# A build-time list scheduler gets landing times by kind of DMA and a new priority table

## Chip, core and metric

The kernel runs on one core of one Trainium2 chip. The metric is the device time of one execution in microseconds; the kernel before was run three times. The chip has five engines that each work through a queue of their own in order: TensorE (PE, with its weight loads PEld), VectorE (DVE), ScalarE (ACT), GpSimd (POOL) and SyncE (SP), which here only starts DMAs.

## What is computed

Three layers in a row. (1) Attention in which a query sees only the keys of its own cluster (the nearest of 16 centroids); B=2, H=8, S=768, D=64. (2) A mixture of experts on the 1536 tokens of width 512: a gate of softmax over 8 experts picks one expert per token. (3) A dense layer 512 to 2048 to 512 with a leaky activation.

```python
mask = q_assign[:, :, :, None] == k_assign[:, :, None, :]
attn = softmax(where(mask, q @ k.T / 8, -1e9)); x = attn @ v          # (1)
e_idx = argmax(x @ w_gate + modality_bias[modality_id])
y = gate_w * (relu(x @ w1[e_idx]) @ w2[e_idx])                          # (2)
h = y @ w_in; out = (max(h, 0) + alpha * min(h, 0)) @ w_out             # (3)
```

## The kernel before

**Who sets the order.** The kernel body doesn't issue instructions. It describes its operations with `S.op(...)` (engines that could do it with an estimated cost on each, buffers read and written, a priority, a tag), and `Sched.run` (lines 194 to 309) plans them when the program is built: it keeps a planned clock for each engine, takes the operation that can start first, and among those of one engine that can start within a small window of each other the one with the lowest priority number. `emit` then issues them in that order. On the chip each engine's queue runs in exactly this order and waits where data is late, so the plan's estimates decide the order and the chip decides the time. `ORDER` (line 79) adds a number to the priority of each tag.

**How the planner sees a DMA.** All DMAs share one planned clock, `dma_free`. In `run` (lines 281 to 286) a DMA that starts at `st` ends its transfer at `max(st + ISSUE, dma_free) + xfer`, with `xfer` given at the operation, and lands 0.13 later; `LEAD` says when SP is free again. Lines 247 and 248 hold back one kind, the loads of q, k and v and of expert weights:

```python
if o.dma is not None and o.dma[1] == "load":
    at = max(at, dma_free - self.back)      # back = 2.13
```

`ISSUE` is 2.37 for a DMA transpose, 1.86 for others on SP and 1.9 for POOL's; `LEAD` is 2.91 and 5.8 (lines 102, 103). A transpose (tag `turn`, xfer 1.91, SP busy 1.43) that starts at st therefore puts `dma_free` at st + 4.28 or later and frees SP at st + 1.5.

**Attention** (`group_prep` line 714, `unit` line 957). Work goes in 8 groups (4 per batch row, 2 heads each). `group_prep` loads q, k, v (line 725, one v buffer `vraw` for all groups), transposes q and k on PE, splits them in high and low parts, finds the clusters, and moves halves between partitions (`move`, line 830: by DMA on SP, or by ACT or POOL). Each group has 12 units of 128 queries: scores on PE (L973), row maximum on DVE (L980), exp on ACT (L992), split of p into two fp16 halves (on ACT, POOL and DVE), a DMA transpose of p on SP (L1026; in the first batch row a third of the units transposes on PE instead), and the product with v on PE (L1034, L1036), which needs the group's v as two fp16 halves: vab (L916), a small chain (L922 to L935), v_hi (L394) and v_lo (L940).

**Experts** (`slot`, line 1340). Tokens are sorted by expert into tiles of 128; 5 tiles of batch row 0 and 8 of row 1 are always run, numbered m = 0 to 12. A tile gathers its rows by an indirect DMA on POOL (L1364), and issues 8 weight loads of 512 KB on SP (L1358) that are skipped on the chip when the expert is that of the tile before. Tiles 0 to 2 run in plain fp32 while attention still occupies memory (L1428 and L1458 with `wst`, about 0.6 us a matmul); they serve PE as filler. From tile 3 on, the weights are split in two parts by ACT and DVE (`whl`). Tile rows go back to memory, and a second gather (`gather`, line 1469, L1474 on POOL) with a scaling (`gated`) brings them in token order for the dense layer.

**Dense layer** (`ffn`, line 1533): the last 280 us, in which PE runs nearly without a gap (L1544, L1572). It is planned by later calls of `run` with an empty priority table (`TAIL`), but with the same DMA costs.

Of the kernel before, what the change touches and what calls it, by code (L numbers as in the profile page):

```python
# [19 lines left out]
P = 128  # L20
# [54 lines left out]
class Op:  # L75
# [16 lines left out]
class Sched:  # L92
# [9 lines left out]
    ISSUE = {"transpose": 2.37, "SP": 1.86, "POOL": 1.9}  # L102
    LEAD = {"transpose": 2.91, "SP": 5.8}
# [98 lines left out]
    def run(self, t0=0.0):  # L202
# [17 lines left out]
        dma_free = pool_till = dve_till = t0  # L220
# [3 lines left out]
        while n_done < total:  # L224
            best = None
            per = {}
            for o in ready:
# [19 lines left out]
                if o.dma is not None and o.dma[1] == "load":  # L247
                    at = max(at, dma_free - self.back)
                ch = None
                for e, c in o.eng.items():  # L250
                    st = max(at, o.at[e], free.get(e, t0))
                    if e == "DVE" and o.two:
                        st = max(st, pool_till - 0.1)
                    if e == "POOL" and not (o.dma and e in (o.dma[3:] or (e,))):
# [25 lines left out]
            moved = o.dma is not None and e in (o.dma[3:] or (e,))  # L280
            if moved:
                xfer, kind, busy = o.dma[:3]
                way = "transpose" if kind == "transpose" else e
                dma_free = max(st + self.ISSUE[way], dma_free) + xfer
                o.end = dma_free + 0.13
                free[e] = st + 1.05 if e == "POOL" else max(st + busy, o.end - self.LEAD[way])
            else:
# [4 lines left out]
                if e == "POOL":  # L292
                    pool_till = free[e]
            ready.remove(o)
# [33 lines left out]
def kernel(  # L328
# [49 lines left out]
    N = dict(s1q=2, s1k=2, s2q=2, s2k=2, p=3, p16=5, pt=4, v16=2, wf_early=2, xs=2, whl=3, whl2=3, whi='A', wlo='D', lead=1, tw=1, wdma=1.0, pss=2, ps1=4, sq=1, bd=1.5, bp=0, ulead=4, pa=2, pb=0, nat=3, hi='*', lo='DP', lo0='PPT', vraw=1, mvp=1, mvb=0, epi=1, rM=2, lob=0.5, idle=40, pace=57, mve='PA', wd=0.3, wa=0.04, wp=0.03, wpl=0.03, wsp=0.07, cs=1, back=2.13, nld=8, lump='cs', mp=90, mps=8, mpn=0, trp=0.5, evp=3, xTs2=0, xtp=9, fl=6, rsh=1, rp0=0, go=-4, so=0, pre=0, fws=5, gs=4, eb=0.8)  # L378
# [267 lines left out]
    def centroid_ops():  # L646
# [3 lines left out]
             w=[craw], dma=(0.3, True, 0.4), tag="centroid_ops1")  # L650
# [27 lines left out]
    def modality_ops():  # L678
# [3 lines left out]
            modality_id.bitcast(I32).rearrange("(b p x) -> p b x", b=B, p=P)), w=[midr], dma=(0.2, True, 0.4), tag="modality_ops1")  # L682
        S.op({"SP": 0.06}, lambda e: nc.sync.dma_start(
            mbias.t.rearrange("p m e -> p (m e)"),
            modality_bias.rearrange("(o m) e -> o (m e)", o=1).to_broadcast([P, 2 * E])), w=[mbias], dma=(0.2, True, 0.4), tag="modality_ops2")
        S.op({"SP": 0.06}, lambda e: nc.sync.dma_start(wg.t, w_gate.rearrange("(k p) e -> p k e", p=P)),
             w=[wg], dma=(0.3, True, 0.4), tag="modality_ops3")
        S.op({"SP": 0.06}, lambda e: nc.sync.dma_start(alp.t, alpha.rearrange("(f p) -> p f", p=P)),
             w=[alp], dma=(0.3, True, 0.4), tag="modality_ops4")
# [1063 lines left out]
```

## Time and profile before

| | us |
|---|---|
| three runs | 753.5, 754.52, 752.79 (median 753.5) |
| the profiled execution | 757.23 |
| its span, first to last instruction | 755.4 |
| busy in it: PE / DVE / ACT / POOL | 689.2 / 512.8 / 410.1 / 306.7 |
[...]

Read it by stages: attention up to about 300 us, experts with a long overlap from 200 to 472, the dense layer from 472 on. PE is busy in 91% of the span, so a change can win only what PE loses in gaps and at the lower clock.

### The profile page before, as it was taken

Reading aid. Unit: us, or ns where it says so; the run is one execution under the profiler, and the core shown is the slowest. Engines: PE = TensorE matmul, PEld = TensorE weight load, DVE = VectorE, ACT = ScalarE, POOL = GpSimd, SP = SyncE. Lnnn points to the kernel's source line nnn. Section 1 sums busy time; section 2 is a strip of 40 time slices with the busy share of each in tenths; the row PEclk is TensorE's granted clock in tenths of the full one; section 3 lists DMA queues with packets and bytes.
Section 4 is the critical chain, followed back from the end, with each engine's and each line's share of the span. In section 5 each row is a group of like instructions: output and inputs, shape, how many; then the busy total and the mean of one; then the engine's idle time right before and its main releaser. Section 6 shows DMA issues by size and latency. Waiting matters only on the chain. (4 is left out here: it accounts for less than half of the span.)

```text
span 755.4 us, 13680 instructions
## 1 busy us (share of the span) xinstructions
PE 689.2 (91%) x5041; PEld 581.3 (77%) x5041; DVE 512.8 (68%) x913; ACT 410.1 (54%) x624; POOL 306.7 (41%) x276
## 2 busy tenths in 40 slices
PE   8878899786998779999898897899999999999997
PEld 7767787785777655568686786799999979999996
DVE  6798888889899741799897694587777533322331
ACT  5778988787889642388776894122222341111112
POOL 4467765573667432012232100365555622222221
PEclk9999999997999989999999899799999999999999
DMA  8498899799999989913755610234433030000002
GB/s 202 127 166 186 142 212 220 131 196 234 222 191 184 174 228 171 364 62 103 267 188 184 206 56 32 85 112 127 152 112 112 28 112 1 1 0 1 1 1 84
DMA packets 167418, 101.58 MB, mean 134 GB/s; under 512 B 133136, under 2 KB 147984, under 8 KB 167344
## 3 DMA queue, kind: packets, MB, share of 16 engines
q1 hardware_dynamic: 165136, 93.63, 51.1%
q0 software_dynamic: 2208, 7.00, 3.6%
q8 instruction: 42, 0.69, 0.4%
q14 instruction: 32, 0.26, 0.1%
HBM read 87.37 MB, written 12.85 MB: 133 GB/s over the span
## 5 line engine op out<-in xcount | busy, mean ns | idle before, releaser
L1572 PE MATMUL ps<-wf,ghl 128*128 128x512 f32 x576 | 140.1, 395 | 2.4 <-POOL ghl L420 1.5
L1572 PEld LDWEIGHTS ps<-wf,ghl 128*128 128x128 f32 x576 | 107.8, 189 | 25.2 <-POOL ghl L420 3.1
L1552 DVE TENSOR_SCALAR m<-ps,alp 128x384 f32<-128x384 f32 x64 | 39.5, 617 | 126.3 <-PE ps L1544 126.3
L392 ACT ACTIVATE ghl<-g 128x384 fp32r<-128x384 f32 x64 | 33.7, 526 | 166.7 <-DVE g L1555 166.7
L420 POOL TENSOR_TENSOR p<-p,p 128x768 f16<-128x768 f32 x57 | 95.7, 1682 | 46.1 <-ACT p L392 42.1
L420 POOL TENSOR_TENSOR ghl<-g,ghl 128x384 fp32r<-128x384 f32 x63 | 67.7, 1075 | 113.9 <-ACT ghl L392 113.9
L420 DVE TENSOR_TENSOR whl<-wst,whl 128x1024 fp32r<-128x1024 f32 x80 | 96.8, 1251 | 12.9 <-ACT whl L392 12.9
L980 DVE TENSOR_REDUCE nm<-pss 128x1 f32<-128x768 f32 x96 | 91.0, 950 | 12.3 <-PE pss L973 10.9
L992 ACT ACTIVATE p<-pss,nm 128x768 f32<-128x768 f32 x96 | 86.1, 899 | 22.1 <-DVE nm L986 7.0
L392 ACT ACTIVATE whl<-wst 128x1024 fp32r<-128x1024 f32 x80 | 82.3, 1057 | 11.3 <-PE ps L1458 6.9
L1034 PEld LDWEIGHTS <-pt 128*128 128x128 f16 x1152 | 60.9, 99 | 21.7 <-DMA pt<-p 12.9
L1034 PE MATMUL ps<-v,pt 128*128 128x65 f16 x1152 | 68.9, 196 | 9.2 <-DMA pt<-p 8.1
L1544 PE MATMUL ps<-x2a,wf 128*128 128x384 f32 x384 | 73.0, 347 | 4.0 <-ACTq L1685 4.0
L1544 PEld LDWEIGHTS ps<-x2a,wf 128*128 128x128 f32 x384 | 70.4, 195 | 5.7 <-ACTq L1685 4.4
L973 PE MATMUL pss<-s1k,s1q 128*128 128x384 f32 x192 | 60.1, 395 | 16.1 <-ACT p L992 15.4
L1544 PE MATMUL ps<-x2b,wf 128*128 128x384 f32 x384 | 69.8, 338 | 0.0
L1544 PEld LDWEIGHTS ps<-x2b,wf 128*128 128x128 f32 x384 | 67.7, 188 | 1.2
L1458 PE MATMUL ps<-whl,hTs 128*128 128x512 f32 x240 | 63.1, 401 | 2.0 <-DVE hTs L420 1.2
L1428 PE MATMUL ps<-whl,xTs 128*128 128x512 f32 x240 | 63.9, 407 | 1.0 <-ACT xTs L392 1.0
L420 POOL TENSOR_TENSOR wf<-tw,wf 128x1024 fp32r<-128x1024 f32 x16 | 40.5, 2532 | 55.8 <-ACT wf L392 55.8
L1458 PEld LDWEIGHTS ps<-whl,hTs 128*128 128x128 f32 x240 | 44.5, 190 | 13.1 <-DVE hTs L420 2.4
L1428 PEld LDWEIGHTS ps<-whl,xTs 128*128 128x128 f32 x240 | 45.3, 193 | 11.3 <-ACT xTs L392 1.4
(246 smaller groups left out, 1182.8 us busy)
## 6 DMA issues: line engine op xcount, KB each, us to landing
wst<-in_moe_w_dram SPq DMA_DIRECT2D x104, 512.0 KB
wst<-in_moe_w_in_dram SPq DMA_DIRECT2D x8, 1024.0 KB
wst<-in_moe_w_out_dram SPq DMA_DIRECT2D x8, 1024.0 KB
ys_d<-ys SPq DMA_DIRECT2D x13, 256.0 KB
raw<-in_k_dram SPq DMA_DIRECT2D x8, 384.0 KB
raw<-in_q_dram SPq DMA_DIRECT2D x8, 384.0 KB
vraw<-in_v_dram SPq DMA_DIRECT2D x8, 384.0 KB
x_d<-xg SPq DMA_DIRECT2D x8, 384.0 KB
```

The costliest lines, as they stand in the source:

```text
L392: nc.scalar.activation(out=out, in_=in_, func=AF.Copy)
L420: ENG[e].tensor_tensor(out=out, in0=a, in1=b, op=ALU.subtract)
L973: nc.tensor.matmul(s.t[:, jj, 0:HS], hd["12"[i], "q"].t[:, h, j, qs], hd["12"[i], "k"].t[:, h, jj], start=(i == 0), stop=(i == 1))
L980: S.op({"DVE": c_dve(SEQ)}, lambda e: nc.vector.tensor_reduce(out=nm.t, in_=s.t[:, :, 0:HS], axis=AX.XY, op=ALU.max, negate=True), r=[s], ...
L992: S.op({"ACT": c_act(SEQ) + 0.04}, lambda e: nc.scalar.activation(out=p.t, in_=s.t[:, :, 0:HS], func=AF.Exp, bias=nm.t), r=[s, nm], w=[p], ...
L1034: nc.tensor.matmul(o[:, c], pv, vv[:, D:VW], start=(i == 0), stop=(i == 2 * C - 1))
L1428: nc.tensor.matmul(hps[jj].t, lhs(xT, a, ci), rhs(ch, w_, cols), start=(ci == 0 and i == 0), stop=(ci == 3 and i == len(parts) - 1))
L1458: nc.tensor.matmul(yp.t, lhs(hT, a, f), rhs(4 + f // 2, w_, slice((f % 2) * 512, (f % 2 + 1) * 512)), start=(f == 0 and i == 0), stop=(f = ...
L1544: nc.tensor.matmul(hp.t[:, 0:HS], wi[:, a, kk, fs], x2b.t[:, bb, kk, sl], start=(n == 0), stop=(n == 3 * KD - 1))
L1552: S.op({"DVE": c_dve(HS) + 0.055}, lambda e: nc.vector.tensor_scalar(out=m.t, in0=hp.t[:, 0:HS], scalar1=0.0, scalar2=alp.t[:, f:f + 1], o ...
L1572: nc.tensor.matmul(view(), gh.t[:, a, tt * P:(tt + 1) * P], wo[:, bb, f % 2, :], start=(f == 0 and a == 0 and bb == 0), stop=(f == NF - 1 ...
```

## The change

It changes the planner's estimates and its table; the operations themselves, their tiles and their arithmetic stay. Each DMA now states four things, `(first, later, kind, busy)`: it lands `first` after its start, or `later` after the DMA ahead of it, and keeps its queue for `busy`. Transposes get a clock of their own that advances by at least `TURN` = 2.15 each. A `move` on POOL may not be planned before the last POOL gather has landed. A DVE operation with two inputs waits for POOL's to end. The expert tiles that really load weights are named in `FRESH`.

```diff
-ORDER = {"chain_a": 5, "chain_g": 4, "chain_i": -20, "chain_r": -16, "chain_s": -43, "chain_v": -0.5, "consts3": 64,
-         "gate_exp": 29, "idle": 52, "logits": -46, "low": -0.5, "mm": 0.12, "mm2": 0.217, "move": 4, "nat_lo": 0.5,
-         "norm_ln": 71, "p_hi": -0.939, "pos_max": -17, "ptr": 1.658, "qk_hi": -0.534, "relu": 3, "row_max": 0.759,
-         "scaled": 1, "shift": -27, "sims_max": -45, "sm": 84, "smm": 2, "smtr": 1.5, "square_sum": 6, "tr": 78,
-         "tr_gather": 22, "v_hi": 1, "v_scale": -1, "w_lo": -0.161, "wb1": 0.5, "wb3": -7.5, "wf_lo": 46,
-         "xt_out": 3.5, "ys_out": 100, "ys_store": 56}
+ORDER = {"avm": 4, "centroid_ops1": -58, "chain_g": 9, "chain_i": -31, "chain_r": -83, "chain_t": 30.091,
+         "chain_v": -5.856, "evac_lo": -44, "idle": 1, "inv_hot": -71, "load_qkv": -83, "low": -4.5, "mm": -0.099,
+         "move": 9, "nat_lo": -8, "norm_exp": -17, "norm_ln": -6, "onehot": -34, "otr": -42, "p_hi": 28, "p_lo": 1,
+         "ptr": 0.197, "qk_hi": 13, "row_max": 3, "scaled": -79, "shift": -101, "sims_out": -52, "sims_scale": 7,
+         "sm": 1, "smm": 0.5, "square": -3, "tr": -2.5, "tr_gather": 19, "tr_slot": -78, "turn": 64, "v_bc": -182,
+         "v_hi": -31, "v_lo": -58, "v_scale": 5, "v_turn": 1, "w_lo": -11, "wb2": 21, "wb3": -18, "wf_lo": 44,
+         "x2_hi": 88}
...
-    ISSUE = {"transpose": 2.37, "SP": 1.86, "POOL": 1.9}
-    LEAD = {"transpose": 2.91, "SP": 5.8}
+    TURN = 2.15
...
                     if e == "DVE" and o.two:
-                        st = max(st, pool_till - 0.1)
+                        st = max(st, pool_till + 0.01)
...
+                        if o.tag == "move":
+                            st = max(st, pool_dma + 0.1, pool_till + 0.1)
...
-                xfer, kind, busy = o.dma[:3]
-                way = "transpose" if kind == "transpose" else e
-                dma_free = max(st + self.ISSUE[way], dma_free) + xfer
-                o.end = dma_free + 0.13
-                free[e] = st + 1.05 if e == "POOL" else max(st + busy, o.end - self.LEAD[way])
+                first, later, kind, busy = o.dma[:4]
+                if kind == "transpose":
+                    turn_free = max(st + busy, turn_free + self.TURN)
+                    free[e] = turn_free + 0.1
+                    first += turn_free - st
+                else:
+                    free[e] = st + busy
+                dma_free = max(st + first, dma_free + later)
+                o.end = dma_free
+                if e == "POOL":
+                    pool_dma = dma_free
...
-              back=2.13, wa=0.04, wp=0.03, wpl=0.03, wsp=0.07
+              back=3.692, wa=0, wp=0.05, wpl=0.04, wsp=0.01
+    FRESH = ((0, 2), (1, 1), (1, 5))
...
-                 dma=((3.44 if always else N["wdma"]) * nl / 2, "load", 0.38)
+                 dma=(*((3.75, 1.6) if always or (b, j) in FRESH else (0.0, 0.0)), "load", 0.39)
```

The `back`/window lines are cut out of one long line of constants. The other estimates, old `xfer` against new `first, later`: q, k, v loads 0.51 / 3.35, 1.5; turn 1.91 / 2.75, 1.4; move on SP 1.42 / 2.85, 0.95 (ACT's cost for a move 0.2 more); mask_k 0.95 / 3.4, 1.5; mask_q 1.26 / 2.6, 0.3; x_store 1.43 / 3.45, 1.45; gather of expert rows 0.9 / 4.3, 0.9; last gather 0.9 / 3.9, 0.9; ys_store, zero rows and out_store 0.75 / 3.4, 0.8; dense weights 3.0 / 4.8, 3.0; the small first loads 0.2 or 0.3 / 3.0, 0.5. Two reciprocals of `chain_h` count 140 instead of 60 elements.

## Rows read from the trace of the kernel before

**Rows 1.** The page's first line: the span of the profiled execution.
```profile
span 755.4 us, 13680 instructions
```

**Rows 2.** Busy time by stage: us, PE, PEld, DVE, ACT, POOL, PEclk, DMA share, GB/s.
```profile
0.00:165.00 165.00, 141.53 (x1697) 125.11 (x1698) 141.23 (x320) 134.64 (x226) 102.00 (x115) 0.98 0.85 176
165.00:200.00 35.00, 27.75 (x285) 23.88 (x283) 30.34 (x87) 26.62 (x44) 15.50 (x14) 0.83 1.09 220
200.00:244.00 44.00, 41.20 (x508) 34.19 (x506) 41.57 (x72) 37.87 (x58) 31.41 (x29) 1.00 1.10 201
244.00:281.00 37.00, 27.41 (x240) 20.28 (x241) 24.17 (x44) 23.02 (x31) 15.21 (x11) 0.86 1.02 201
281.00:327.00 46.00, 44.64 (x336) 24.54 (x332) 21.21 (x97) 16.08 (x24) 6.67 (x5) 1.00 0.88 233
327.00:411.00 84.00, 79.85 (x379) 63.20 (x378) 78.41 (x78) 68.86 (x88) 23.12 (x14) 1.00 0.45 156
411.00:424.00 13.00, 8.77 (x32) 6.86 (x31) 6.17 (x7) 7.11 (x10) 0.83 (x1) 0.74 0.90 326
500.00:756.00 256.00, 248.87 (x1260) 225.23 (x1259) 117.81 (x157) 55.22 (x90) 93.88 (x76) 1.00 0.17 58
```

**Rows 3.** What PE waited for, 244 to 281 us: total, times, longest.
```profile
PE pss L973 <- ACT p L992: 4.1, 6, 1.3
PE ps L1034 <- DMA pt<-p: 3.3, 2, 3.1
```

**Rows 4.** Timeline of SP's queue, 214 to 297 us: start, us, what, count.
```profile
214.09 20.37 SPq L1026 DMA_TRANSPOSE pt<-p  x10
...
235.51 6.79 SPq L1026 DMA_TRANSPOSE pt<-p  x3
...
244.89 19.93 SPq L1026 DMA_TRANSPOSE pt<-p  x9
...
267.44 1.21 SPq L725 DMA_DIRECT2D vraw<-in_v_dram  x1
268.87 5.10 SPq L1358 DMA_DIRECT2D wst<-in_moe_w_dram  x8
280.98 15.46 SPq L1026 DMA_TRANSPOSE pt<-p  x8
```

**Rows 5.** Timelines of DVE, ACT and PE: the v path and tile 0's second half.
```profile
218.06 1.15 DVE L940 SCALAR_TENSOR_TENSOR v<-vraw,vsc,v 128x384 f16<-128x384 f32 x2 [0.68 <-ACT v L394]
...
272.04 0.84 ACT L916 ACTIVATE vab<-vraw 128x768 bf16<-128x768 f32 x1 [2.00 <-DMA vraw<-in_v_dram]
...
277.03 1.15 DVE L940 SCALAR_TENSOR_TENSOR v<-vraw,vsc,v 128x384 f16<-128x384 f32 x2 [0.85 <-ACT v L394]
...
273.39 2.08 PE L1458 MATMUL ps<-wst,hT 128*128 128x512 f32 x2
```

**Rows 6.** Timelines of POOL, SP, ACT and PE around the gap at 412 us.
```profile
408.72 0.96 POOL L1474 DMA_INDIRECT yg<-ys_d,posc  x1 [0.30 <-issue]
...
403.02 16.17 SPq L1358 DMA_DIRECT2D wst<-in_moe_w_dram  x8
...
415.38 0.72 ACT L394 ACTIVATE yg<-yg,gate 128x512 f32<-128x512 f32 x1 [5.00 <-DMA yg<-ys_d,posc]
...
408.17 2.20 PE L1428 MATMUL ps<-whl,xTs 128*128 128x512 f32 x9
...
416.63 1.12 PE L1451 MATMUL ps<-ident,hb 128*128 128x128 f32 x4 [4.23 <-ACT hb L1437]
417.40 4.19 PE L1428 MATMUL ps<-whl,xTs 128*128 128x512 f32 x9
```

**Rows 7.** Busy time by stage as in rows 2: two stretches of real weight loading.
```profile
309.00:315.00 6.00, 6.00 (x16) 2.62 (x14) 5.28 (x32) 0.80 (x2) 0.00 (x0) 1.00 1.04 406
...
411.00:417.00 6.00, 1.77 (x9) 1.20 (x8) 1.19 (x2) 1.62 (x3) 0.83 (x1) 0.90 1.00 386
```

**Rows 8.** The tile yg: all twelve last gathers, issue to landing.
```profile
DMA to landing us min/median/max: 3.3/3.9/6.6
```

More of the change, by code (lines that the diff above doesn't have):

```diff
@@ L219, in run @@
         free = {}
-        dma_free = pool_till = dve_till = t0
+        dma_free = turn_free = pool_dma = pool_till = dve_till = t0
         ready = [o for o in ops if o.ndep == 0]
@@ L246, in run @@
                     continue
-                if o.dma is not None and o.dma[1] == "load":
+                if o.dma is not None and o.dma[2] == "load":
                     at = max(at, dma_free - self.back)
@@ L252, in run @@
                     if e == "DVE" and o.two:
-                        st = max(st, pool_till - 0.1)
-                    if e == "POOL" and not (o.dma and e in (o.dma[3:] or (e,))):
+                        st = max(st, pool_till + 0.01)
+                    if e == "POOL" and not (o.dma and e in (o.dma[4:] or (e,))):
                         st = max(st, dve_till)
+                        if o.tag == "move":
+                            st = max(st, pool_dma + 0.1, pool_till + 0.1)
                     cost = st + c + o.bias.get(e, 0.0)
@@ L279, in run @@
             o.on = e
-            moved = o.dma is not None and e in (o.dma[3:] or (e,))
+            moved = o.dma is not None and e in (o.dma[4:] or (e,))
             if moved:
-                xfer, kind, busy = o.dma[:3]
-                way = "transpose" if kind == "transpose" else e
-                dma_free = max(st + self.ISSUE[way], dma_free) + xfer
-                o.end = dma_free + 0.13
-                free[e] = st + 1.05 if e == "POOL" else max(st + busy, o.end - self.LEAD[way])
+                first, later, kind, busy = o.dma[:4]
[9 more added lines that the diff above has]
+                    pool_dma = dma_free
             else:
@@ L293, in run @@
                     pool_till = free[e]
+                    if o.tag == "move":
+                        free[e] += 0.12
             ready.remove(o)
@@ L377 @@
     BIG = float(2.0 ** 60)
-    N = dict(s1q=2, s1k=2, s2q=2, s2k=2, p=3, p16=5, pt=4, v16=2, wf_early=2, xs=2, whl=3, whl2=3, whi='A', wlo='D', lead=1, tw=1, wdma=1.0, pss=2, ps1=4, sq=1, bd=1.5, bp=0, ulead=4, pa=2, pb=0, nat=3, hi='*', lo='DP', lo0='PPT', vraw=1, mvp=1, mvb=0, epi=1, rM=2, lob=0.5, idle=40, pace=57, mve='PA', wd=0.3, wa=0.04, wp=0.03, wpl=0.03, wsp=0.07, cs=1, back=2.13, nld=8, lump='cs', mp=90, mps=8, mpn=0, trp=0.5, evp=3, xTs2=0, xtp=9, fl=6, rsh=1, rp0=0, go=-4, so=0, pre=0, fws=5, gs=4, eb=0.8)
+    N = dict(s1q=2, s1k=2, s2q=2, s2k=2, p=3, p16=5, pt=4, v16=2, wf_early=2, xs=2, whl=3, whl2=3, whi='A', wlo='D', lead=1, tw=1, pss=2, ps1=4, sq=1, bd=1.5, bp=0, ulead=4, pa=2, pb=0, nat=3, hi='*', lo='DP', lo0='PPT', vraw=1, mvp=1, mvb=0, epi=1, rM=2, lob=0.5, idle=40, pace=57, mve='PA', wd=0.3, wa=0, wp=0.05, wpl=0.04, wsp=0.01, cs=1, back=3.692, nld=8, lump='cs', mp=90, mps=8, mpn=0, trp=0.5, evp=3, xTs2=0, xtp=9, fl=6, rsh=1, rp0=0, go=-4, so=0, pre=0, fws=5, gs=4, eb=0.8)
+    FRESH = ((0, 2), (1, 1), (1, 5))
     W_EARLY = N["wf_early"]
@@ L830, in move @@
             n = G * HS
-            ways = {"SP": 0.65, "POOL": c_pts(n), "DVE": c_dve(n, True), "ACT": c_act(n)}
+            ways = {"SP": 0.65, "POOL": c_pts(n), "DVE": c_dve(n, True), "ACT": c_act(n) + 0.2}
             S.op({x: c for x, c in ways.items() if x[0] in N["mve"] + "S"}, fn,
-                 r=[(src, x) for x in K(sp_, sy)] + (zeros if z else []), w=[(dst, x) for x in K(part, y)], dma=(1.42, True, 0.6, "SP"), bias=mv_bias, tag="move")
+                 r=[(src, x) for x in K(sp_, sy)] + (zeros if z else []), w=[(dst, x) for x in K(part, y)], dma=(2.85, 0.95, True, 0.65, "SP"), bias=mv_bias, tag="move")
         a, a2, kk, kk2 = (pt[x] for x in (("1", "q"), ("2", "q"), ("1", "k"), ("2", "k")))
@@ L1026, in unit @@
             S.op({"SP": 0.06}, lambda e: nc.sync.dma_start_transpose(out=p16t(pt), in_=p16.t.rearrange("p a s -> p (a s)")),
-                 r=[(p16, 0), (p16, 1)], w=[pt], dma=(1.91, "transpose", 1.43), tag="turn")
+                 r=[(p16, 0), (p16, 1)], w=[pt], dma=(2.75, 1.4, "transpose", 1.43), tag="turn")
         a = accumulator()
@@ L1360, in slot @@
             S.op({"SP": 0.6 if c0 == 0 else 0.06}, load, r=[(ei, b), (fl, b)], w=[(wst, c0 + x) for x in range(nl)],
-                 dma=((3.44 if always else N["wdma"]) * nl / 2, "load", 0.38), prio=p0 - 5,
+                 dma=(*((3.75, 1.6) if always or (b, j) in FRESH else (0.0, 0.0)), "load", 0.39), prio=p0 - 5,
                  deps=[] if pace is None else [units[pace + c0]], tag="w_load")
@@ L1476, in gather @@
             in_offset=bass.IndirectOffsetOnAxis(ap=pos.t[:, T:T + 1], axis=0)),
-            r=[(pos, b)] + ([ysd] if tiles is None else [(ysd, x) for x in tiles]), w=[yg], dma=(0.9, False, 0), tag="rows")
+            r=[(pos, b)] + ([ysd] if tiles is None else [(ysd, x) for x in tiles]), w=[yg], dma=(3.9, 0.9, False, 1.05), tag="rows")
         S.op({"DVE": c_dve(DM, True), "ACT": c_act(DM) + 0.1, "POOL": c_pts(DM)},
```

32 lines of the change are left out of this document (16 added, 16 removed).

## The prediction

> **What bounds the kernel now.** I began with the span, 755.4 us [rows 1], then cut it into stages by busy time [rows 2]. In the dense layer PE is busy 248.9 of the last 255.4 us at full clock, so no order of instructions can win much there. The loss is ahead of it. From 0 to 165 us PE stands idle 23.5 us, but DVE is 86% and ACT 82% busy: three engines share that bound. [...] From 200 to 244 everything is full (idle 2.8). From 244 to 281, the end of attention, PE idles 9.6 us, the clock averages 0.86, and now DVE (65%), ACT (62%) and POOL (41%) are slack too: this stretch waits for data and not for an engine. From 281 to 327 PE is full with expert tiles 0 to 2. From 411 to 424 PE idles 4.2 us at clock 0.74, again with all engines slack.
>
> For the slack stretch at 244 to 281 I read who waits: PE waits 4.1 us for exps and 3.3 us for transposed p [rows 3]. The reason is on SP's queue [rows 4]. Transposes run back to back: 10 in 20.4 us, 3 in 6.8, 9 in 19.9. Only then, at 267.4, does the v of the last group start loading, and behind it at 268.9 come eight expert loads. Then no transpose is issued until 281. DVE finished the last use of the v buffer at 219.2 [rows 5], so this load stood some 48 us behind transposes. What hung on it: vab at 272.0, v_lo at 277.0 to 278.2, and only then the products with v that empty the p buffers. Tile 0's second half, the filler that PE lacked, starts at 273.4, right behind the expert loads.
>
> **Why the old plan did this, and what the change does to it.** By the old rule a transpose at st puts the DMA clock at st + 4.28 or later and frees SP 2.78 ahead of that clock, while a load may start only 2.13 ahead of it. So while another transpose is ready, it always starts 0.65 us before the load may: loads starve. By the new rule, in a run of transposes, SP is free at the transposes' clock + 0.1, the DMA clock is that + 2.75, and a load may start 3.692 ahead, thus 0.94 before the transposes' clock. Load and transpose can start together, and the table decides: load_qkv at -83 and the expert loads of tile 0 at 95 against a `turn` of at least 57 + 64 = 121 behind unit 57. Loads go first. This I can work out from the code; how far the whole plan then moves I can not.
>
> **The terms.**
> (a) The last v and tile 0's loads go some 45 us earlier. Moved are one load of 384 KB and up to four real loads of 512 KB (tile 0's second half; the other four of the eight are tile 1's, skipped if the expert stays). Each passes up to 22 transposes on SP. No row shows such a load between two transposes; eight real loads elsewhere ran at 406 GB/s [rows 7], from which I estimate 1.3 us for 512 KB and 1.0 for 384 KB: together 6.2 us by which the transposes behind them come later. They give that back, since at 267.4 to 281.0 the queue no longer stops for 13.5 us. I cost the move itself at nothing, covered by those 13.5 us; without that cover it costs 6.2. The gain is what PE gets back in 244 to 281: 9.6 us idle, and at clock 0.86 at most 0.14 x 37 = 5.2 us, together 14.8 at most, nothing at least. Filler is there, since tile 0's second half and tile 1 wait with their inputs gathered. Some waits for exps stay (4.1 us [rows 3], the pace of two score buffers). I take 10: the idle time less half those waits, and half of the clock's share.
> (b) The gap at 412. ACT had `gated` in its queue ahead of the relu `hb`; the gather for it left POOL at 408.7 and ACT got going at 415.4, PE at 416.6 after 4.23 us [rows 6]. The nine L1428 matmuls behind it took 4.19 us instead of the 2.20 of the same group at 408.2, at the lower clock. So the stall is worth 4.2 + 2.0 = 6.2 and some tenths. The gather was late because eight real loads of tile 10 ran beside it [rows 6] at 386 GB/s [rows 7]. The old plan lands a gather at 1.9 + 0.9 + 0.13 = 2.93 and takes 0.5 a load; the new one 3.9, and 1.6 for a load of a tile in `FRESH`, which names tile 10. All gathers took 3.3 to 6.6 us, median 3.9 [rows 8]: the new figure is right for the median and still 2.7 short here. So I expect part of it: 3, between 0 (the same pile-up) and 6.2.
> (c) TURN = 2.15 against steps of 1.91: the rows show 2.04 and 2.21 a transpose [rows 4], so plan and chip no longer drift apart by about a quarter us per transpose in long runs. Its worth is in (a); alone I count nothing.
> (d) Moves on POOL behind gathers, DVE behind POOL, dearer reciprocals and ACT moves: these remove waits of POOL and DVE that PE does not see, or make the plan more cautious. Cost nothing where PE is covered by 82 to 86% busy neighbours, as before; bounds with (e).
> (e) The table for the rest of attention, 0 to 244: preparation of the next group (tr from 78 to -2.5, sm from 84 to 1, norm_ln from 71 to -6) becomes urgent. No row shows that order. Bounds: half of the idle 23.5 + 7.3 gained (15), or as much lost. I take 0, as nothing in the rows says which sign.
> (f) The dense layer: gathers and weight loads planned later, PE's full queue [rows 2] covers it: 0; without that cover one gather, 3.9 [rows 8].
>
> Sum: 10 + 3 = 13 us. The profiled execution took 757.2 (span 755.4), 3.7 above the median of 753.5; taking the same 13 off the median gives **740.5**.
>
> **Rivals.**
> *The hole only moves.* If the transposes and loads together, and not their order, set the end of attention, then each load put forward pushes the transposes behind it. For it: DMA share is 1.09, 1.10 and 1.02 from 165 to 281 [rows 2]. Against it: in the 13.5 us without transposes only five real loads, about 6.2 us, were moved. Then a gain of 13.5 - 6.2 = 7 on SP remains, of which PE, busy with tiles 1 and 2 until 327 anyway, keeps maybe half: 750.
> [...]
> *A transpose is no limit at all.* Here 22 transposes of 384 KB went at 2.04 to 2.26 us each [rows 4], so they do limit: 48 units of the second batch row need about 100 us of SP.
> [...]
> *Slower.* The place is DVE in 0 to 244: the prep of the next group, now urgent, is issued as a block ahead of row maxima, ACT's exps follow late, and PE, with two score buffers, waits for them as it does in 244 to 281 for 4.1 us [rows 3]. If each of the 7 later groups loses 2.6 us to this, that is 18 us against the 13: 753.5 + 5 = 758.5. It decides from 13 / 7 = 1.9 us a group on. For it: DVE at 86% and 94% in 0 to 165 and 200 to 244 [rows 2] has little room. Against it: the planner weighs DVE's queue with costs that the change mostly leaves alone.
> *The change does not do what it says:* the same starved load in spite of the rule, because another wait holds it: 753.5.
>
> **How the numbers follow.** Chances: forecast 0.52; hole moves 0.20; slower 0.21; no effect 0.07. A measurement of this kernel tells 0.2% (1.5 us) from no change. Faster: all of the first, 0.17 of the second, 0.02 of the last, together 0.71. Same: 0.02 and 0.05 and 0.02 at the edge of the slower case, 0.09. Slower: 0.19 of that case and 0.01 of the second, 0.20. The low end takes (a) at 12, (b) at 6 and 7 of (e): 753.5 - 25 = 728.5. The high end, 757, takes in the hole that moves, no effect, and the milder part of the slower case; the rest of it, about 0.15, and some 0.05 below 728.5 stay out. The forecast's own case with 7 us of (e) either way and (a) down to 6 is 729 to 751.
>
> **What would show it.** Right, if the last group's vraw load starts within some 10 us of the last use of that buffer, no gap of over 5 us stands between transposes before the last one, tile 0's second half runs before the last unit, and PE's idle time in the last 40 us of attention falls from 9.6 to under 4. Right for (b), if no single wait of PE for `hb` exceeds 2 us. Wrong, if the dense layer starts less than 5 us earlier than before, or if waits for exps in 0 to 244 have grown by more than the 13 us. The dense layer itself should keep its length within 2 us.

## The result and the profile after

The changed kernel takes 764.2 us (median of 4, 760.23 to 765.02) against 753.28 beside it: ratio 1.0132, interval [1.0095, 1.0169]. It is slower by 10.9 us; 740.5 was forecast. In the runs further down a few executions fell in a slower state and are left out of times and ratios, so a_shared, for one, stands at 776.11 here where a recorded text has 778.8 for all four. The profiled execution took 765.02, its span 763.2. All later lines of the code stand 11 lower: the product with v is L1045, the transposes L1037, scores L984, exps L1003, loads of q, k, v L736, expert loads L1369.

Busy time by stage, the columns and most of the stretches of [rows 2] (PEclk is the granted clock of PE as a share of full speed):

```profile
0.00:165.00 165.00, 139.00 (x1694) 124.30 (x1694) 141.98 (x320) 133.50 (x229) 94.98 (x103) 0.97 0.96 192
165.00:200.00 35.00, 25.16 (x280) 22.04 (x279) 32.24 (x86) 21.23 (x36) 14.97 (x14) 0.80 1.07 211
200.00:244.00 44.00, 36.23 (x402) 28.22 (x401) 31.28 (x63) 29.70 (x43) 20.43 (x20) 1.00 1.14 208
244.00:281.00 37.00, 29.54 (x303) 21.63 (x300) 22.61 (x43) 19.88 (x27) 17.37 (x15) 0.91 1.00 198
281.00:327.00 46.00, 41.02 (x361) 26.72 (x360) 17.16 (x51) 18.82 (x28) 10.92 (x8) 0.96 1.02 242
...
500.00:763.00 263.00, 257.06 (x1303) 232.98 (x1301) 122.10 (x166) 56.79 (x93) 111.57 (x81) 1.00 0.18 61
```

The stretch that the prediction wanted to mend, 244 to 281, did get better: PE idles 7.5 us there instead of 9.6, at clock 0.91 instead of 0.86. The loss stands where nothing was expected: from 200 to 244 PE idles 7.8 us instead of 2.8, from 281 to 327 5.0 instead of 1.4, from 165 to 200 9.8 instead of 7.3, and from 0 to 165 26.0 instead of 23.5. From 0 to 327 together that is 56.1 us of idle time instead of 44.5, about as much more as the kernel lost. The DMA share of 0 to 165 rose from 0.85 to 0.96. Attention ends later: its last product with v runs at 315.4 us instead of 300.5, and the dense layer begins at 480.8 instead of 471.9.

What PE waited for over the whole of attention, 0 to 335 us (total, times, longest), first before, then after:

```profile
PE pss L973 <- ACT p L992: 15.4, 23, 1.9
PE ps L1034 <- DMA pt<-p: 8.1, 10, 3.1
```

```profile
PE ps L1045 <- DMA pt<-p: 30.1, 25, 3.1
PE pss L984 <- ACT p L1003: 9.7, 13, 1.4
```

Waits for exps fell by 5.7 us; waits for transposed p rose by 22.0. So the transposes come late, and SP's queue shows how (start, us, what, count; the counterpart of [rows 4]):

```profile
228.48 1.42 SPq L1369 DMA_DIRECT2D wst<-in_moe_w_dram  x2
230.01 3.34 SPq L1037 DMA_TRANSPOSE pt<-p  x1
233.41 0.68 SPq L428 DMA_DIRECT2D s1k<-s1k  x1
234.18 1.25 SPq L428 DMA_DIRECT2D s2q<-s1q  x2
235.53 5.77 SPq L1037 DMA_TRANSPOSE pt<-p  x2
241.40 0.60 SPq L428 DMA_DIRECT2D s1k<-s1k  x1
242.10 1.56 SPq L1037 DMA_TRANSPOSE pt<-p  x1
243.71 1.30 SPq L736 DMA_DIRECT2D vraw<-in_v_dram  x1
245.23 0.38 SPq L1369 DMA_DIRECT2D wst<-in_moe_w_dram  x1
245.72 2.69 SPq L1037 DMA_TRANSPOSE pt<-p  x1
248.51 0.84 SPq L1085 DMA_DIRECT2D x_d<-xg  x1
249.45 4.45 SPq L1037 DMA_TRANSPOSE pt<-p  x2
```

The runs of 9 and 10 transposes are gone; the longest has 5. Seven transposes take from 230.0 to 253.9, 3.4 us each, because loads, moves and a store stand between them. In the second batch row the median distance from one transpose's start to the next is 2.84 us; before it was 2.00 (44 transposes from 165 us on in each).

Two things arrived as planned by the new rules. The last v starts to load at 243.71 instead of 267.44, and its path ends earlier (ACT's vab, then DVE's v_lo; [rows 5]):

```profile
248.65 0.84 ACT L927 ACTIVATE vab<-vraw 128x768 bf16<-128x768 f32 x1 [1.18 <-DMA vraw<-in_v_dram]
...
264.48 1.14 DVE L951 SCALAR_TENSOR_TENSOR v<-vraw,vsc,v 128x384 f16<-128x384 f32 x2
```

And one thing not foreseen: the planner now sends twice as many moves through SP. The first two kinds of move in the helper's line (engine, tiles, count, then duration of the issue in ns and first and last start), before and then after:

```profile
L417 SPq DMA_DIRECT2D s1k<-s1k x6: 590/610/733, 10.0 to 153.0; - x6
L417 SPq DMA_DIRECT2D s2q<-s1q x5: 603/648/857, 10.8 to 118.5; - x5
```

```profile
L428 SPq DMA_DIRECT2D s1k<-s1k x15: 590/652/822, 8.2 to 241.4; - x15
L428 SPq DMA_DIRECT2D s2q<-s1q x12: 591/604/912, 9.1 to 234.8; - x12
```

With the other kinds it is 40 moves of 192 KB by DMA instead of 20, nine of them in the second batch row, where before had none. When a DMA from SP has landed the trace doesn't tell; it does so for some of POOL's only.

### The profile page after: what moved, and what is told of

It is laid out like the page before. It is cut to its first block, busy times and chain, and to the rows that moved or that the text cites. A ratio compares the mean times of both kernels' runs of the same rounds, so it can differ in the third digit from the quotient of the medians.

```text
span 763.2 us, 13672 instructions
## 1 busy us (share of the span) xinstructions
PE 684.0 (90%) x5041; PEld 578.9 (76%) x5041; DVE 508.9 (67%) x914; ACT 402.3 (53%) x617; POOL 306.7 (40%) x261
## 5 line engine op out<-in xcount | busy, mean ns | idle before, releaser
L431 POOL TENSOR_TENSOR ghl<-g,ghl 128x384 fp32r<-128x384 f32 x63 | 77.5, 1230 | 114.8 <-ACT ghl L403 114.8
L1003 ACT ACTIVATE p<-pss,nm 128x768 f32<-128x768 f32 x96 | 85.6, 898 | 27.5 <-DVE nm L997 17.8
L1045 PE MATMUL ps<-v,pt 128*128 128x65 f16 x1152 | 69.2, 198 | 31.5 <-DMA pt<-p 30.1
L1045 PEld LDWEIGHTS <-pt 128*128 128x128 f16 x1152 | 61.0, 100 | 47.6 <-DMA pt<-p 42.1
L984 PE MATMUL pss<-s1k,s1q 128*128 128x384 f32 x192 | 61.8, 404 | 9.8 <-ACT p L1003 9.7
L1439 PE MATMUL ps<-whl,xTs 128*128 128x512 f32 x240 | 65.8, 412 | 1.0 <-DVE whl L431 0.7
```

The costliest lines, as they stand in the source:

```text
L431: ENG[e].tensor_tensor(out=out, in0=a, in1=b, op=ALU.subtract)
L984: nc.tensor.matmul(s.t[:, jj, 0:HS], hd["12"[i], "q"].t[:, h, j, qs], hd["12"[i], "k"].t[:, h, jj], start=(i == 0), stop=(i == 1))
L1003: S.op({"ACT": c_act(SEQ) + 0.04}, lambda e: nc.scalar.activation(out=p.t, in_=s.t[:, :, 0:HS], func=AF.Exp, bias=nm.t), r=[s, nm], w=[p], ...
L1045: nc.tensor.matmul(o[:, c], pv, vv[:, D:VW], start=(i == 0), stop=(i == 2 * C - 1))
L1439: nc.tensor.matmul(hps[jj].t, lhs(xT, a, ci), rhs(ch, w_, cols), start=(ci == 0 and i == 0), stop=(ci == 3 and i == len(parts) - 1))
```

## The experiments

Each ratio is to runs of the kernel before on the same chip, with its 95% interval. "D" is the theory that transposes and all other DMAs draw on one limit, so that each DMA put among transposes delays them (in the first runs it is tried on the moves alone, as "M", against "T", that the table puts loads and everything else ahead of them); "F" is its rival, that the old order just happens to suit the chip and any other order loses a per cent.

**1. The moves, taken away and added.** In the changed kernel's order the 40 DMA moves are done in place by POOL and ACT in turn (a_moves_off); in the order of before, every second of the first 40 moves that ACT or POOL do goes through SP, 40 by DMA in all (b_moves_on); and in the order of before, the 20 DMA moves go to POOL and ACT (b_moves_off).

```diff
-            o.fn(o.on)
+            e = o.on
+            if o.tag == "move" and e == "SP":
+                self.nm = getattr(self, "nm", 0) + 1
+                e = "POOL" if self.nm % 2 else "ACT"
+            o.fn(e)
```

> The order of the changed kernel is kept as planned; only the 40 moves that it does by DMA on SP are done in the same places by POOL and ACT in turn. Theory M (the 20 added moves by DMA take time on the DMA engines that the transposes need, and the planner does not see it): PE's waits for transposed p fall from 30 us to under 18, the last product with v comes 8 us or more sooner than at 315 us, and the time falls to 752 to 759. Rival T (transposes are late because the table puts loads and everything else ahead of them): waits for transposed p stay over 25 us and the time stays at 764 or rises by the 33 us of work that POOL and ACT get.

Measured: 766.38, ratio 1.014 [1.0077, 1.0204]. PE's waits for transposed p fell to 17.1 us, but those for exps rose to 19.8: the wait changed its name, and nothing was regained. The last product came at 319.4, later than 315.4. M had the waits right and the time wrong, T the reverse.

> The order of the kernel before is kept; every second of the first 40 moves that POOL and ACT do is done by DMA on SP in the same place, so that 40 moves go by DMA as in the changed kernel. Theory M: waits of PE for transposed p rise from 9 us to 15 or more and the time rises by 5 to 12 us, to 758 to 766. Rival T: within 3 us of 753.3, since the order of SP's queue puts nothing else ahead of a transpose.

Measured: 774.22, ratio 1.0248 [1.0215, 1.0281], 18 us above before, with 17.6 us of waits for transposed p: M had the sign, and T's "within 3 us" fell, but the loss is larger than M had it.

> The mirror of the run that doubled them: the order of before, its 20 DMA moves done in place by POOL and ACT in turn. 20 more DMAs had cost 11 us. Theory D (what a DMA move costs the transposes is given back when it goes, and POOL and ACT have room): 5 to 10 us below before. Rival E (in the first batch row POOL and ACT are as short as the DMA engines, so a move costs the same wherever it is put outside its planned place): within 3 us of before or up to 8 above, with PE's waits for exps up by 5 us or more from 15.4 and those for transposed p down from 8.1.

Measured: 755.8, ratio 1.0008 [0.9975, 1.004]. The time is E's: nothing is given back. Waits for transposed p fell to 6.6 and those for exps rose to 17.9, half of what E had, so its reason isn't shown.

**2. Price of a DMA alone.** To price the DMA without touching POOL and ACT, each of the 20 DMA moves of before is followed by a copy of the same 192 KB to a scratch array in the chip's memory (b_moves_twice; a move itself stays on the core); then nine such copies stand behind moves of the second batch row's groups (b_copies_row1).

```diff
                 if e == "SP":
-                    dma(e, rd(o), i)
+                    dma(e, rd(o), i); nmv.append(0); nc.sync.dma_start(scr[:, len(nmv) - 1], i)
```

> The price of 20 more 192 KB DMAs on SP without any change elsewhere: the order of before, each of the 20 moves that go by DMA is followed by a copy of it to a scratch array in memory. Theory D (they share the transposes' limit): SP and the DMA engines lose 1 to 1.5 us for each, about half of it covered in the first batch row, total 8 to 15 us above before, and PE's waits for transposed p grow from 8 us to 15 or more. Theory F (the old table fits the old plan and any other order loses a per cent, DMAs are not the cause): within 2 us of before.

Measured: 765.28 against 754.08, ratio 1.0162 [1.0131, 1.0193]: 11.2 us for 20 copies, 0.56 each (0.5 to 0.7 by the interval). The waits after it (0 to 335 us):

```profile
PE ps L1034 <- DMA pt<-p: 16.3, 16, 3.1
PE pss L973 <- ACT p L992: 13.5, 21, 2.5
```

Waits for transposed p doubled, 8.1 to 16.3, and those for exps did not grow. D held, F's "within 2 us" did not.

> The order of before; behind nine of the second batch row's moves, which POOL and ACT do, SP copies the same 192 KB to a scratch array. The changed kernel has nine moves by DMA in this row, before has none. Theory D (the DMA engines, at a share above 1 there, set the row's pace): 1 us or more for each, total 8 to 12 above before, the row's length (last x store of the first row to last of the second, 139.8 us) up by about as much, PE's waits for transposed p up from 8.1 to over 14. If the row has slack for them: within 3 us of before.

Measured: 764.58 against 755.89, ratio 1.0132 [1.0061, 1.0202]: 8.7 us for nine, 1.0 each. The interval allows 0.5 to 1.7, so that a copy costs more here than in the first row isn't shown. How it is paid is only partly as D had it. The second row itself grew by 5.0 us (144.9 against 139.9) and the first by 4.7, since three of the copies start before 160 us; the waits for transposed p stayed at 8.7, and those for exps rose to 19.4. One cause is the source buffer: ACT waited 4.7 us for copies that still held it (the profile's list of who waited for the copies):

```profile
who waited for it (us, times):
  ACT s1q L392: 4.7, 2
```

**3. Term (a) alone.** In the order of before, only on SP's queue, the last group's v and tile 0's four w2 loads are put forward among the transposes. Every other queue is the same instruction by instruction.

```diff
+EARLY = {1247: 208, 1575: 212, 1576: 216, 1577: 220, 1578: 224}
-        order = sorted(ops, key=lambda o: (o.start, o.idx))
+        order = sorted(ops, key=lambda o: (EARLY.get(o.idx, o.start) if t0 == 0 else o.start, o.idx))
```

> Term (a) alone: the order of before, and only on SP's queue five DMAs move forward past transposes (the last group's v, 13 places, and tile 0's four w2 loads); every other queue is unchanged. As the prediction had it (the starved load is what opens the hole): last v load starts before 232 us instead of 267, no gap over 5 us between transposes before the last one, attention's last product ends about 9 us earlier (291 instead of 300), total 8 to 10 us below before. Theory D (transposes and all other DMAs share one limit): the hole closes, but the transposes behind the loads come 5 to 6 us later, so attention ends 3 to 7 us earlier and the total is 0 to 4 us below before. If it is slower than before by over 2 us, both fall.

Measured: 759.62 against 754.08, ratio 1.0074 [1.0055, 1.0093], 5.5 us slower. Both stated gains fell. SP's queue:

```profile
221.54 1.02 SPq L725 DMA_DIRECT2D vraw<-in_v_dram  x1
222.68 4.32 SPq L1026 DMA_TRANSPOSE pt<-p  x2
227.20 0.66 SPq L1358 DMA_DIRECT2D wst<-in_moe_w_dram  x1
227.98 4.58 SPq L1026 DMA_TRANSPOSE pt<-p  x2
232.77 0.42 SPq L1358 DMA_DIRECT2D wst<-in_moe_w_dram  x1
233.30 4.81 SPq L1026 DMA_TRANSPOSE pt<-p  x2
...
271.28 1.81 SPq L1026 DMA_TRANSPOSE pt<-p  x1
275.76 1.79 SPq L1358 DMA_DIRECT2D wst<-in_moe_w_dram  x4
284.55 15.34 SPq L1026 DMA_TRANSPOSE pt<-p  x8
```

From the v at 221.54 to the transpose at 233.30, four transposes and three loads take 11.8 us; at 2.04 to 2.21 a transpose [rows 4] the transposes alone would take 8.2 to 8.8. So three loads cost 3.0 to 3.6 us, 1.0 to 1.2 each: what the prediction had estimated (1.0 and 1.3). But the hole stayed. With the v loaded 46 us earlier, no transpose is issued from 273.1 to 284.6, 11.5 us against 13.5 before. The hole was not made by the late load alone: ACT, DVE and PE run their queues in the planned order, with the v path and tile 0's products at their old places, and these lie in the hole (PE's matmul of v's scale, L922, runs at 278.44, tile 0's w2 products from 278.65). Nor was the hole idle time. Busy time of before by stage in those 14 us (columns as in [rows 2]):

```profile
267.00:274.00 7.00, 2.91 (x10) 1.87 (x11) 5.36 (x10) 3.39 (x5) 2.14 (x2) 0.89 1.03 274
274.00:281.00 7.00, 7.00 (x43) 4.03 (x42) 2.67 (x8) 3.00 (x5) 1.61 (x2) 0.62 0.54 196
```

In its first half the DMA engines carry the loads (share 1.03), in its second PE is full with tile 0. PE idles 4.1 us here, and in the second half it works at a granted clock of 0.62, worth at most another 0.38 x 7 = 2.7 us, an estimate from that clock. That is all PE could win, and only if all the queues moved.

**4. Rules and table, crossed.** Old rules with `back` = 3.692 alone, so that loads start ahead of transposes (b_back); new rules with the old table (a_old_table); old rules with the new table (b_new_table).

```diff
-              back=2.13
+              back=3.692
```

> The kernel before with back = 3.692 alone, so loads are held back less; costs and table as before. My term (a) (the hole at the end of attention closes when the last v comes in time): v of the last group loads before 235 us, time 743 to 750. Rival (the hole only moves, and a table fitted to the other plan loses what is won): last v before 235 us too, time 751 to 757.

Measured: 761.86, ratio 1.0079 [1.0051, 1.0108], above both ranges. The last v loads at 226.9, no gap over 5 us is left behind 200 us, and attention's last product comes 3 us earlier (297.3): as far as that, term (a) came true. But tiles 0 to 2 were done 15 us later (first matmul on `whl` at 341.7 instead of 326.7). The execution that was profiled took 755.72, the least of the five, so its trace shows little of the loss.

> The changed planner with the old table; 29 moves by DMA on SP instead of 40. Theory M (moves by DMA set the loss): between the two kernels by the count of moves, 756 to 761. Theory T (the new table's order makes the loss): 753 or less. If the new estimates by themselves are what hurts: 764 or more.

Measured: 763.67, ratio 1.0082 [1.0043, 1.0122]; 25.7 us of waits for transposed p. M and T both fell; it lies next to the third case, that the new estimates hurt with the old table too.

> Old rules with the new table alone. Its plan ends at 731.7 against 716.5 for before. If chip times follow the plans: 768 (15 us above before). Theory D: loads wait behind transposes again, as the old rules make them, so PE's waits for transposed p stay under 20 us although 28 moves go by DMA; total 760 to 770. Theory F: as bad as any other mix of table and rules, 758 to 768, with no single wait standing out.

Measured: 764.93, ratio 1.0155 [1.0137, 1.0173]; 13.9 us of waits for transposed p. D and F both allow this, so the run doesn't decide between them.

**5. Is any other order worse?** Two small perturbations of the old table under the old rules, b_shift0 (the first pair of lines) and b_three (the second).

```diff
-"shift": -27,
+"shift": 0,
...
-"tr_gather": 22,
+"tr_gather": 36.4, "p_lo": -0.22, "v_bc": -42,
```

> A small perturbation of the old plan under the old rules: one number of the old table (shift -27 to 0). 742 operations move by over 3 us, 54 change engine, still 20 moves by DMA; the plan ends 3.1 us later. If chip times follow plans made by the old rules: 2 to 5 us above before. Theory F (the old order happens to suit the chip, and any other order loses a per cent whatever it promises): 6 to 12 us above before, as in the runs with new rules or new table.

Measured: 755.29, ratio 1.0022 [0.9985, 1.0059].

> A second perturbation under the old rules: three numbers of the old table. 773 operations move by over 3 us, 25 change engine, 21 moves by DMA; the plan ends 1.4 us later. If chip times follow plans: 0 to 4 us above before. Theory F: 6 to 12 us above.

Measured: 759.11, ratio 1.0065 [1.0026, 1.0104]. The first can't be told from before; its interval (1 us below to 4.5 above) takes in most of what the plan had and nothing of F's. The second falls between the two. F as stated falls: with the plan's end 3 us later, 742 operations moved and no loss that can be measured, a different order need not cost a per cent.

**6. Does the plan keep its promise?** The planner states an end when the program is built. Set beside the chip's median:

```text
kernel            plan's end   chip    behind the plan
before              716.5      753.3        36.8
b_back              728.1      761.9        33.8
b_new_table         731.7      764.9        33.2
b_shift0            719.6      755.3        35.7
b_three             717.9      759.1        41.2
a_old_table         726.6      763.7        37.1
changed kernel      708.2      764.2        56.0
```

Six orders end 33 to 41 us behind their plans; the changed kernel 56. (The kernel before took 753.3 to 756.5 beside these runs, so some 3 us in the last column mean nothing.) Its plan promised 8 us over before and was wrong by some 19 (56.0 less 36.8). By the plan's own times the error arises in the second batch row: the stretch from the 43rd to the 81st transpose is planned at 94.4 us and takes 122.1, while before it was planned at 98.2 and took 105.7. The suspect is the new clock for transposes: it moves by `TURN` for each transpose and by nothing for a move, load, store or gather. That the new table was tuned on this clock is inferred: under the new rules it promises 708.2, the old table 726.6. Two replans tell this apart: DMA taken from the ways of a move (a_nosp, the first part of the diff), and the transposes' clock pushed by every other DMA (a_shared, the second).

```diff
-            S.op({x: c for x, c in ways.items() if x[0] in N["mve"] + "S"}, fn,
+            S.op({x: c for x, c in ways.items() if x[0] in N["mve"]}, fn,
...
                     free[e] = st + busy
+                    if kind != "load" or later:
+                        turn_free = max(turn_free, st) + later
```

> The changed kernel's planner, but DMA is no longer among the ways of a move, so the whole plan is made for 64 moves on POOL (28) and ACT (36). It promises an end at 722.3, where the changed kernel's own plan promised 708.2. If the chip follows the plans: 14 us above the changed kernel, 778. Theory D (the DMA moves are what the changed kernel loses by): PE's waits for transposed p fall from 30 us to under 12 and the total to 750 to 757. Theory F: 760 to 770 again, with waits for exps in place of those for transposed p.

Measured: 760.03, ratio 1.0059 [1.0027, 1.0091], 37.7 behind its plan: about half of the loss comes back though the plan is 14 us worse. But waits for transposed p stayed at 21.2 us, not under 12, and the stretch from the 43rd to the 81st transpose, planned at 91.2, still took 110.4. The moves are not the whole of it.

> The changed kernel, planned with a transposes' clock that every other DMA also pushes by its own later. Theory D: the plan becomes honest in the second batch row: the stretch from the 43rd to the 81st transpose, planned at 94 and run in 122 us in the changed kernel, now runs within 10 us of its plan, PE's waits for transposed p fall from 30 us to under 15, and the total falls below the changed kernel's by 5 us or more, though the table was not tuned for this clock. Theory F: the stretch still runs 15 us or more over plan or the time lost appears as other waits, total 760 to 770.

Measured: 776.11, ratio 1.0295 [1.0225, 1.0364], 33.6 behind its plan. The plan is honest again: the stretch from the 43rd to the 81st transpose, planned at 126.6, took 135.3 in the profiled execution (781.76), within the stated 10, and the waits for transposed p are 6.1 us. But with a table made for another clock it is a bad plan: those for exps are 25.0, and the time rose instead of falling.

**7. Tuning on either clock.** The same random search of the table (5000 steps, the planner's end as its only measure) on a_nosp's rules, whose clock is blind, and on a_shared's. It is one search on each, and the second also has DMA among the ways of a move.

> The changed kernel's rules without DMA among the ways of a move, and the table searched anew on exactly these rules (5000 random steps); the plan now ends at 704.7, below the changed kernel's 708.2. If the DMA moves are what the changed plan gets wrong, the chip ends 33 to 41 us behind this plan as in the other kernels: 738 to 746, 10 to 16 us below before. If the cause is a table tuned on a transposes' clock that sees no other DMA, tuning finds the same error again: 52 to 60 behind the plan, 757 to 765, and most of the drift arises in the second batch row, with PE's waits for transposed p at 20 us or more.

Measured: 753.63, ratio 0.9958 [0.9917, 0.9998]; 48.9 behind the plan, 3 short of the range that was stated for the blind clock and 8 beyond the other; the time, too, lies between the two that were stated. The search won 17.6 us of plan and the chip kept some 6 of them. The second batch row is half of the drift and not most of it: 21.4 us over plan from the 43rd to the 81st transpose, 20.0 ahead of them. The waits, 0 to 335 us:

```profile
PE ps L1045 <- DMA pt<-p: 22.9, 12, 6.2
PE pss L984 <- ACT p L1003: 13.9, 18, 2.1
```

No move goes by DMA here, and still it is the transposed p that is late (22.9 us of waits): loads, masks and stores still stand among the transposes, which come 2.70 us apart at the median from the 43rd to the 81st.

> The same search on the planner whose transposes' clock is pushed by every other DMA; plan 724.7 (742.5 before the search), 13 moves by DMA. If a table tuned on the blind clock is the cause, this tuned plan stays honest: 33 to 41 us behind its plan, 758 to 766, and 12 us or more below the untuned 778.8. If any tuning makes a plan over-promise: 52 or more behind, 777 to 785.

Measured: 742.17 against 755.89, ratio 0.9838 [0.9775, 0.99]: 33.9 us below the untuned plan on the same clock, and 17.5 behind the plan, closer than any other and better than either theory had said. It beats both kernels.

> The kernel of the run a_shared_tuned once more, for its interval: 1.2 to 2% below before, if the first measurement was no accident; 0 to 1% if it was.

Measured: 742.06 against 755.84, ratio 0.9805 [0.9768, 0.9842]. The gain holds. Waits (0 to 335 us) and stages of this run:

```profile
PE pss L986 <- ACT p L1005: 12.4, 18, 1.5
PE ps L1047 <- DMA pt<-p: 6.2, 9, 1.6
```

```profile
200.00:244.00 44.00, 41.63 (x378) 30.13 (x376) 31.45 (x67) 32.65 (x50) 23.48 (x22) 1.00 1.07 214
244.00:281.00 37.00, 36.74 (x299) 24.70 (x299) 19.12 (x33) 22.69 (x33) 14.32 (x11) 1.00 1.08 243
281.00:327.00 46.00, 44.92 (x475) 35.75 (x471) 36.20 (x49) 33.13 (x45) 16.92 (x11) 1.00 0.84 161
```

From 244 to 281, where before lost 9.6 us and clock, PE now idles 0.3 us at clock 1.00. Attention ends later than before (last product at 321.8) and it doesn't matter: the plan, which has transposes 3.2 us apart from the 43rd on (the chip 3.1), puts the fp32 tiles between the units, and the first matmul on `whl` runs at 293.3, while attention still goes on, instead of 326.7.

> The search on the shared clock carried on by 8900 steps: plan 719.1 instead of 724.7, 10 moves by DMA. If the shared clock is honest under tuning, the chip follows: 18 us behind the plan as the run before, 737, some 4 us below it. If further tuning spends the promise as it did on the blind clock, 742 or more, 23 us or more behind the plan.

Measured: 747.58 against 755.84, ratio 0.9888 [0.9854, 0.9922], 28.5 behind the plan. Another 5.6 us of promise cost 5.5 us of time. Tuning on the better clock spends the promise too, only later, and mostly elsewhere, as the plans' own times show: of the 11 us that it ends further behind than a_shared_again, 9 arise behind the last transpose and 5 from the 43rd to the 81st. Below is the time that a stretch took in the profiled execution less the time planned for it; the last column is the median distance between the starts of two transposes from the 43rd to the 81st:

```text
                      us over plan, by transposes        distance,
                  1st to 43rd  43rd to 81st  behind     plan / chip
before                7.3           7.5       20.2      1.91 / 1.98
a_old_table          17.5          12.9        4.3      2.15 / 2.11
changed kernel       11.2          27.7       15.2      2.17 / 2.90
a_nosp               14.8          19.2        2.7      2.19 / 2.69
a_nosp_tuned         20.0          21.4        3.1      2.28 / 2.70
a_shared             11.1           8.7       16.1      3.24 / 3.12
a_shared_again        5.1           4.7        3.2      3.18 / 3.12
a_shared_tuned2       3.9           9.6       11.9      3.29 / 3.05
```

The transposes' clock bears on the second column: 4 to 10 us with the shared clock, 6 to 10 in the five kernels planned by the old rules, 12.9 with the blind clock and the old table, 19 to 28 with tables tuned on the blind clock. The total alone misleads. By it a_nosp looks as honest as before, which it is not in this column. And of the 19 us by which a_shared_again ends closer to its plan than before does, 17 stand behind the last transpose, where this clock has nothing to plan; why that part keeps its plan better stays open.

## Why the prediction was wrong

**(a) The step that failed first.** It called the move of the loads free, "covered by those 13.5 us". The mechanism ahead of it was right: by the new rule loads start before waiting transposes, the last v by 24 us, and the price of a load, 1.0 to 1.2 us, was as estimated. The cover was not there. The run that moves these loads alone shows the bare price (5.5 us slower, where 6.2 without cover had been named) and a hole that stays, because it lies in the order of the other queues. The prediction had read an empty stretch of SP's queue as lost time; PE's loss inside it was 4.1 us of idle time and at most 2.7 of clock. In the changed kernel the hole did shrink (the longest gap between transposes before the last one is 5.4 us, at 272.8), and the 2.1 us that PE won in 244 to 281 were paid back several times around it. Of the prediction's own signs, tile 0's second half did run before the last unit (from 239.7), but the last v loaded 16 us behind the last use of its buffer and not 10, and PE's idle time in the last 40 us of attention is 6.4 and not under 4. (It was 5.9 there before: the 9.6 of the prediction is that of 244 to 281, and attention ended at 300.5.)

**(c) The step that failed most.** `TURN` was taken as worth nothing by itself, since 2.15 agrees with 2.04 and 2.21 in runs of transposes. It does agree there, but the change also cut the transposes loose from the clock of the other DMAs, and the prediction did not ask what a planner does with a resource that it believes free. It puts loads and moves among the transposes, and the transposes came 2.84 us apart. From the 43rd to the 81st they took 16.4 us longer than before (122.1 against 105.7), more than the whole loss. The runs show this clock as the cause of the broken promise: with the clock shared, a plan is as honest as by the old rules (33.6 us behind, and 17.4 to 28.5 after tuning); with the blind clock, a table tuned on it promises 12 us (without DMA moves, 48.9 less 36.8) to 19 us (with them) too much. Slow transposes by themselves are not the loss: in the fastest kernel they come 3.1 us apart, but there the plan reckons with it and has other work for PE. That the faster kernel owes its time to the clock and not to a luckier search is likely and not shown, with one search on each clock.

**(d) Not cost-free.** The dearer ACT move and the wait behind gathers were called "more cautious". But the changed planner sends 20 more moves to SP. Rules and table share in this: 20 moves go by DMA before, 29 with the new rules and the old table, 28 with the old rules and the new table, 40 with both; which single estimate does it was not tried. Twenty more DMAs of that size cost 11.2 us in the first batch row, nine cost 8.7 around the second. In the changed kernel these prices don't simply add up: POOL and ACT were relieved in exchange, and giving the moves back to them in place regained nothing. How much of the 10 us belongs to the moves and how much to the loads stays open: a_moves_off regained nothing, a_nosp about half.

**(b)** failed as a gain. A gather still lands late behind real loads, and ACT's `hb` stands behind `gated` (PE, ACT, POOL, SP; the counterpart of [rows 6]):

```profile
427.62 1.11 PE L1462 MATMUL ps<-ident,hb 128*128 128x128 f32 x4 [6.49 <-ACT hb L1448]
...
426.36 0.72 ACT L405 ACTIVATE yg<-yg,gate 128x512 f32<-128x512 f32 x1 [6.15 <-DMA yg<-ys_d,posc]
...
419.61 0.96 POOL L1485 DMA_INDIRECT yg<-ys_d,posc  x1 [0.30 <-ACT whl L403]
...
411.72 9.57 SPq L1369 DMA_DIRECT2D wst<-in_moe_w_dram  x6
```

The stall moved from 412 to 421 us and grew from 4.2 to 6.5; the gather took 6.7 us from 419.6 to ACT's start, where the plan has 3.9.

**(e), (f).** The first batch row ended 3.1 us later (166.5 instead of 163.4), inside the bounds. The dense layer kept its length (282.3 against 283.5), as the prediction said.

**The rivals.** "The hole only moves" had the right mechanism: a load put among transposes pushes them back, here by 1.0 to 1.2 us. The rival was wrong in still leaving a gain. The slower rival had the right sign and 758.5, but the wrong place: it named waits for exps in 0 to 244, and these fell. The stated sign of failure, a dense layer that starts less than 5 us earlier, came: it started 8.9 later.

**Not tried:** the changed order with only its loads put back behind transposes (its products wait for that v, so it would measure another thing), and a search of the same length on the old rules, which would tell what searching alone is worth.

## What to carry to other kernels

A gap in a queue is worth what the bounding engine loses in it (here 4.1 us of idle time and at most 2.7 of clock in a gap of 13.5), and it is filled only if every queue that was ordered around it moves as well (with the loads alone moved, 11.5 us of it stayed). When a planner gets better estimates for each kind of work but loses the link between kinds that share a resource, tuning will find the missing link and spend it: compare promise and chip for several orders, stretch by stretch and not by the total alone, and distrust the one that promises most. Here one shared clock and a new search made the kernel 1.6 to 2% faster than before, and the same search carried on gave 1.1%.

## What the runs showed of the hardware

A DMA of 192 KB kept SP's queue for about 0.6 us (before, the medians of the kinds of move are 0.59 to 0.67). Each of 20 added ones in the first batch row cost 0.56 us of the whole kernel. Nine around the second row, where the DMA share is above 1 (1.05 to 1.12 from 165 to 281 us), cost 1.0 us each, with an interval of 0.5 to 1.7.

DMA transposes of 384 KB followed each other every 2.04 to 2.21 us in runs of 9 and 10. With moves, loads and stores among them the median distance was 2.84 us.

Landing times were no constants of a kind here. The indirect gathers of expert rows landed after 4.3 us at the median before (thirteen) and after 7.2 in the changed kernel (the seven that its trace times), whose planner has 4.3 for all of them. So the landing times of a table hold for the order that they were read from.
